# Merging two partial attentions in SBUF on GpSimd, with the opening's work and loads in a new order

## The chip, the cores and the metric

The kernel runs on one core of a Trainium2 chip. The core has five engines, each of which executes its own stream of instructions in order: PE (TensorE, matrix products into PSUM), ACT (ScalarE, functions such as Exp), DVE (VectorE), POOL (GpSimd) and SP (SyncE, which here issues every DMA). They meet only through semaphores. The metric is the time of one launch on the device, in microseconds.

## The reference, cut to what matters

Two identical layers, each an attention block and a feed-forward block, on x of 2048 rows by 512 columns in bfloat16:

```python
def _A_ref(x, wqkv, wo):              # H = 32 heads of 16
    q, k, v = split(x @ wqkv)
    p = softmax(q @ k.T / 4)
    return (p @ v) @ wo
def _B_ref(x, w1, b1, w2, b2):        # feed-forward width 1376
    y = layernorm(x)
    return gelu(y @ w1 + b1) @ w2 + b2

x = x + A(layernorm(x)); x = x + B(layernorm(x))
x = x + A(layernorm(x)); x = x + B(layernorm(x))
```

The heavy part is Exp over 32 heads x 2048 x 2048 scores in each of the two layers.

## The kernel before

**A planner writes the streams.** Nothing is looped on the chip. `Sched` and `Prog` run while the program is built: jobs are Python generators that yield tasks (an engine, a priority, a list of instructions with resources read and written, and a modelled duration). The planner keeps a modelled clock, takes for each engine the ready task of lowest priority number, and appends it to that engine's stream. The order so found is fixed; on the chip an engine that meets a wait stops, with everything behind it. A DMA is modelled with a short issue time and 2 us to landing unless given otherwise. Where the model sees a gap on PE, `fill_pe` puts in dummy matmuls of zeros (L853).

**Stages.** x is cut into 16 tiles of 128 rows and 4 chunks of 512 (`qc`). The layers are L = 1 and 3. For each row tile `job_qkv_tile` normalizes x into `xn` (L657), turns it by a DMA transpose into `xnT` (L684), and multiplies it by the three column blocks of `wqkv` (L709). K goes through a DMA transpose into `KT` (L697), V into `V` by ACT or DVE (L736, L738), Q into the DRAM buffer `q_scr` (L777). Squares and sums of q and k (L752, L753), and five short GpSimd instructions for a square root (L763 to L767), fill a bound on the scores into a spare column of q. In the tiles 0 to 3 of L = 1 ("start") the first 128 columns of q also go by a DMA transpose to `qraw` (L775). `job_qt` scales a `qraw` block to `QT` (L823).

**Attention.** `flow_scores` goes through segments: a chunk of queries, a group of four heads (`hg`, 8 of them), and a set of key tiles. A group of score tiles of 128 keys x 512 queries is written to PSUM (L915), ACT takes Exp over two or three of them into `PT` (L921), and PE multiplies `V` with them into one accumulator bank (`ACCB`, L1040). In the wide mode, which begins with the second pass over chunk 0, some tiles have their Exp done on DVE instead: `take_d` gives one to the DVE lane (L932, then `job_d`, L999 to L1002). `job_segend` turns the accumulator into `accT` (two buffers, L1067).

**Two parts.** Chunk 0 of each layer is done in two passes over the eight head groups, so that Exp can begin before all keys exist: in L = 1 over key tiles 0 to 3 and then 4 to 15, in L = 3 over 0 to 11 and then 12 to 15. After the first pass, 16 x 17 float32 numbers of each of 128 partitions are stored from `accT` into the DRAM buffer `m_scr` (L1082). After the second they are loaded into `MA` (one buffer, L1092), scaled by a weight `dw`, which is an Exp of the difference of two bounds (L1090), and added to `accT`, both on DVE (L1093, L1094). Then come the reciprocal (L1097), the product into `ob` (L1102), a transpose into `OT` (L1104), the output projection with `wo` (L1121) and the feed-forward block (`job_post`, `job_ffn`).

**The opening.** `build_startup` puts down the x and `wqkv` loads in one go (five DMAs of x and three of `wqkv`, L563 and L566), constants, and the zero and one columns of all six q/k buffers on GpSimd. `build_startup_late` then appends to GpSimd's stream the fills of `wo`, `V`, `vst`, `ob`, `b1s`, `w2` and `g10` (L606 to L613) ahead of anything a job puts there, and submits the loads of `wo`, `w1`, `w2`, b1 and b2 to SP at the lowest priority (L618 to L631). b1 is loaded element by element into a column layout.

Of the kernel before, what the change touches and what calls it, by code (L numbers as in the profile page):

```python
# [8 lines left out]
BF16 = mybir.dt.bfloat16  # L9
# [398 lines left out]
DTAIL = 16  # L408


class Builder:
# [35 lines left out]
    def alloc(self, es):  # L447
# [8 lines left out]
        self.b1s = t("b1s", [128, NFC], BF16)  # L456
# [31 lines left out]
        self.MA = t("MA", [128, 1, 16, 17], F32)  # L488
# [4 lines left out]
        self.sq = t("sq", [128, 64, 16], BF16)  # L493
# [19 lines left out]
        self.m_scr = nc.dram_tensor("m_scr", [2, 8, 128, 272], F32, kind="Internal").ap()  # L513
# [11 lines left out]
        pl["qk"] = Pool(range(6))  # L525
        pl["vst"] = Pool(range(2))
        pl["xn"] = Pool(range(3))
        pl["xnT"] = Pool(range(3))
        pl["sq"] = Pool(range(1))
        pl["n2"] = Pool(range(2))  # L530
        pl["accT"] = Pool(range(2))
        pl["MA"] = Pool(range(1))
        pl["ob"] = Pool(range(2))
# [10 lines left out]
    def qkr(self, s):  # L544
        return ("qk", s) if s < 2 else ("h", s - 2)
# [10 lines left out]
    def build_startup(self):  # L556
# [25 lines left out]
        pool(lambda e: e.iota(self.ioe[:, :, :], [[-4, 8], [-1, 4]], base=0, channel_multiplier=1, allow_small_or_imprecise_dtypes=True), [("ioe",)])  # L582
        dve(lambda e: e.memset(self.zw[:, :], 0.0), [], [("zw",)], 0.2)
        dve(lambda e: e.memset(self.ps[:, ACCB, :], 0.0), [], [("ps", ACCB)], 0.6)
        for b in range(6):
            qv = self.qks(b).rearrange("p k (h c) -> p (k h) c", c=32)
            pool(lambda e, qv=qv: e.memset(qv[:, :, 16:32], 0.0), [self.qkr(b)], 0.7)
            pool(lambda e, b=b: e.memset(self.qks(b)[:, 1, :].rearrange("p (h c) -> p h c", c=32)[:, :, 16:17], 1.0), [self.qkr(b)], 0.2)
# [11 lines left out]
    def build_startup_late(self):  # L600
        NFC = self.NFC
        n0 = self.now0
        nc = self.nc
        nfull = NFC - 1
        pool = lambda fn, writes, dur=0.4: n0("pool", I(fn, [], writes, dur))
        pool(lambda e: e.memset(self.wo[:, :, :].rearrange("p a b -> p (a b)").bitcast(F32), 0.0), [("wo0",)], 2.5)  # L606
        vv = self.V[:, :, :, :, :].rearrange("p g k h d -> p (g k h) d")
        pool(lambda e: e.memset(vv[:, :, 16:17], 1.0), [("V", hg, kb) for hg in range(8) for kb in range(16)], 1.0)
        pool(lambda e: e.memset(self.vst[:, :, :].rearrange("p s (h d) -> p (s h) d", d=17)[:, :, 16:17], 1.0), [("vst", 0), ("vst", 1)], 0.4)
        pool(lambda e: e.memset(self.ob[:, :, :], 0.0), [("ob", 0), ("ob", 1)], 1.0)  # L610
        pool(lambda e: e.memset(self.b1s[:, :], 0.0), [("b1z",)])
        pool(lambda e: e.memset(self.w2[:, nfull, :], 0.0), [("w2z",)], 0.6)
        pool(lambda e: e.memset(self.g10[:, :], 0.0), [("g10",)], 0.6)  # L613
        self.S_.submit(Task("dve", 4.0, [I(lambda e: e.memset(self.g10[96:97, :], 1.0), [], [("g10",)], 0.5)]))
        wor = self.A_wo.rearrange("(g h d) n -> h d g n", h=4, d=16)
        late = []
        for hp in range(4):
            late.append(I(lambda e, hp=hp: e.dma_start(self.wo[32 * hp:32 * hp + 16, :, :], wor[hp]), [("wo0",)], [("wo", hp)], 0.1))  # L618
        late.append(I(lambda e: e.dma_start(self.w1[:, :, :], self.B_w1.rearrange("(c p) n -> p c n", p=128)), writes=[("w1",)], dur=0.1, lat=5.0))
        late.append(I(lambda e: e.dma_start(self.w2[:, 0:nfull, :], self.B_w2[0:nfull * 128, :].rearrange("(c p) n -> p c n", p=128)), writes=[("w2", 0)], dur=0.1, lat=5.0))  # L620
        late.append(I(lambda e: e.dma_start(self.w2[0:self.FLAST, nfull, :], self.B_w2[nfull * 128:self.F, :]), [("w2z",)], [("w2", 1)], 0.1))
        late.append(I(lambda e: e.dma_start(self.w2[96:97, nfull, :], self.B_b2.rearrange("(o n) -> o n", o=1)), [("w2z",)], [("w2", 2)], 0.1))
        b1v = self.B_b1

        def ld_b1a(e):
            with nc.allow_non_contiguous_dma(reason="tiny bias load"):
                return e.dma_start(self.b1s[:, 0:nfull], b1v[0:nfull * 128].rearrange("(c p) -> p c", p=128))

        def ld_b1b(e):
            with nc.allow_non_contiguous_dma(reason="tiny bias load"):  # L630
                return e.dma_start(self.b1s[0:self.FLAST, nfull:nfull + 1], b1v[nfull * 128:self.F].rearrange("(p c) -> p c", c=1))  # L631
        late.append(I(ld_b1a, [("b1z",)], [("b1s", 0)], 0.1))
        late.append(I(ld_b1b, [("b1z",)], [("b1s", 1)], 0.1))
        for k, x in enumerate(late):
            self.S_.submit(Task("sp", 4.0, [x]), cb=(lambda: self.S_.mark(("b1ld",))) if k == len(late) - 1 else None)
        self.S_.when([("b1ld",)], lambda: self.S_.submit(Task("dve", 4.0, [I(lambda e: e.tensor_copy(out=self.b1c[:, :], in_=self.b1s[:, :]), [("b1s", 0), ("b1s", 1)], [("b1c",)], 0.2)])))
# [38 lines left out]
    def job_qkv_tile(self, L, tt, slot, i, left, prio, what):  # L675
        S_ = self.S_
        xr = yield ("get", "xn")
        xnr = self.xn[:, xr, :]
        yield self.ln_apply(tt, slot, i, xnr, ("xn", xr), prio)
# [3 lines left out]
        xs = yield ("get", "xnT")  # L683
        yield self.dma(lambda e: e.dma_start_transpose(self.xnT[:, xs, :, :], xnr), [("xn", xr)], [("xnT", xs)], prio, 0.9)  # L684
        S_.release("xn", xr)
        direct = (L == 1) or tt >= 12
        start = (L == 1 and tt < 4)
        qs = yield ("get", "qk")
        QR = self.qkr(qs)
# [5 lines left out]
        def kstore():  # L695
            if direct:
                yield self.dma(lambda e: e.dma_start_transpose(self.KT[:, :, tt * 128:(tt + 1) * 128], self.qks(qs)[:, 1, :]), [QR], [("kt", hg, tt) for hg in range(8)], prio, 1.75)  # L697
            else:
                yield self.dma(lambda e: e.dma_start(self.k_scr[tt * 128:(tt + 1) * 128, :], self.qks(qs)[:, 1, :]), [QR], [("kscr", tt)], prio)
            S_.mark(("ks", L, tt))  # L700
# [6 lines left out]
        def mm(which, b):  # L707
            for c0 in (0, 2):
                yield Task("pe", prio, [I(lambda e, c=c: e.matmul(self.ps[:, b, :], lhsT=self.xnT[:, xs, c, :], rhs=self.wqkv[:, c, which * 512:which * 512 + 512], start=(c == 0), stop=(c == 3)),  # L709
                                          [("wqkv", which), ("xnT", xs)], [("ps", b)], 0.216, [("ps", b)]) for c in (c0, c0 + 1)])  # L710
        yield ("ready", "pe", [("xnT", xs)])
        if "k" in what:
            b = yield ("get", "mb")
            yield from mm(1, b)
            yield Task("dve", prio, [I(lambda e, b=b: e.tensor_copy(out=kdst, in_=heads(self.ps[:, b, :])), [("ps", b)], [QR], 0.68)])
            S_.release("mb", b)
            S_.spawn(kstore(), prio)
        if "q" in what:
            b = yield ("get", "mb")
            yield from mm(0, b)  # L720
            qsrc = heads(self.ps[:, b, :])
            if start:
                yield Task("act", prio, [I(lambda e: e.activation(out=qdst, in_=qsrc, func=ACTF.Copy, scale=0.25 * YU), [("ps", b)], [QR], 0.65)])
            else:
                yield Task("dve", prio, [I(lambda e: e.tensor_scalar(out=qdst, in0=qsrc, scalar1=0.25 * YU, scalar2=None, op0=ALU.mult), [("ps", b)], [QR], 0.68)])
            S_.release("mb", b)
# [18 lines left out]
        S_.release("xnT", xs)  # L745
        ss = yield ("get", "sq")
# [5 lines left out]
        yield Task("dve", prio, [I(lambda e: e.tensor_tensor(out=self.sq[:, h0:h1, :], in0=v4, in1=v4, op=ALU.mult), [QR], [("sq",)], 0.12 + 0.0085 * N)])  # L752
        yield Task("dve", prio, [I(lambda e: e.tensor_reduce(out=self.n2[:, ns, h0:h1], in_=self.sq[:, h0:h1, :], axis=AX.X, op=ALU.add), [("sq",)], [("n2", ns)], 0.12 + 0.017 * N)])  # L753
# [4 lines left out]
        if "q" in what:  # L758
# [9 lines left out]
                                        [RA], [QR], 0.4)])  # L768
# [3 lines left out]
        if "q" in what:  # L772
            li = L // 2
            if start:
                yield self.dma(lambda e: e.dma_start_transpose(self.qraw[:, 0:1, tt * 128:(tt + 1) * 128], self.qks(qs)[:, 0, 0:128]), [QR], [("qraw", 0)], prio, 0.25)  # L775
                S_.mark(("q0", tt))
            yield self.dma(lambda e: e.dma_start(self.q_scr[li, tt * 128:(tt + 1) * 128, :], self.qks(qs)[:, 0, :]), [QR], [("qscr", L, tt)], prio)  # L777
            S_.mark(("qst", L, tt))
# [534 lines left out]
```

## Time and profile before

| what | value |
|---|---|
| time of a launch, median of 3 | 1919.53 us (1917.12 to 1921.61) |
| the profiled launch | 1914.84 us |
| its span, first to last instruction | 1913.1 us |
| mean granted TensorE clock | 0.983 |
| PE, DVE, POOL busy | 91%, 84%, 6% of the span |

The profiled launch is one execution; its span lacks 1.74 us of that launch's own time, and the launch lies 4.69 us under the median of the timed runs. A row of the timeline reads: start, duration, engine, line, instruction, tile written and tile read, count, and in brackets the engine's idle time before it and what ended it. SPq rows are DMA issues. In the chain of waits a DMA row runs from issue to landing. Matmul ends are modelled, and a matmul's duration overlaps with its neighbours'.

### The profile page before, as it was taken

What the parts mean: (1) busy time and instruction counts of PE and PEld (TensorE: products, weight loads), DVE (VectorE), ACT (ScalarE), POOL (GpSimd) and SP (SyncE); (2) the same over time, 40 slices, a digit from 0 to 9 for tenths busy, and PEclk for the clock granted to TensorE, in tenths of its full rate; (3) what the DMA queues carried; (4) which work ended last, traced back from release to release, by engine and by line L of the source; (5) the groups of instructions that cost most, each with busy time, mean ns of one, the idle gap of its engine ahead of it and who ended that gap; (6) DMA issues with size and microseconds to landing.
All of it is one profiled execution on the core that took longest, in us unless ns stands there. A gap on an engine that the chain in (4) does not pass through costs nothing.

```text
span 1913.1 us, 32397 instructions
## 1 busy us (share of the span) xinstructions
PE 1743.7 (91%) x13118; PEld 671.1 (35%) x13118; DVE 1600.0 (84%) x2511; ACT 1734.6 (91%) x1531; POOL 122.2 (6%) x230
## 2 busy tenths in 40 slices
PE   2879889999999999999999989999999999999997
PEld 1223333333333333333333324333333333333334
DVE  4659889989997999879988878888999798997982
ACT  1669889998999999999999989999999999999992
POOL 4102110001000020001000001000000000000000
PEclk9989999999999999999999989999999999999999
DMA  7791120102000110001611141100000000000000
GB/s 186 93 77 34 40 51 23 23 4 59 20 7 15 31 48 7 15 7 51 102 32 26 16 50 40 30 17 17 4 7 18 12 9 7 7 18 14 1 2 22
DMA packets 184515, 59.38 MB, mean 31 GB/s; under 512 B 167121, under 2 KB 178226, under 8 KB 184370
## 3 DMA queue, kind: packets, MB, share of 16 engines
q1 hardware_dynamic: 184370, 57.31, 16.1%
q8 instruction: 107, 1.75, 0.4%
q14 instruction: 38, 0.31, 0.1%
HBM read 10.92 MB, written 17.53 MB: 15 GB/s over the span
## 4 chain that ended last, share of the span: by engine, by line
ACT 51%; PE 34%; DVE 6%; DMA 6%; POOL 1%; issue 1%; SPq 0%; POOLq 0%; DVEq 0%
ACT PT L921 48%; PE ps L915 10%; PE ps L1040 6%; PE ps L853 5%; PE ps L1153 4%; PE ps L1121 3%; PE ps L709 3%; PE ps L1187 3%; DMA xnT<-xn 2%; ACT h L1180 2%; DVE dt L932 1%; DMA yT<-xn 1%; DMA b1s<-in_B_b_dram 1%; DVE de L1002 1%; DMA MA<-m_scr 1%
## 5 line engine op out<-in xcount | busy, mean ns | idle before, releaser
L921 ACT ACTIVATE PT<-ps 128x1024 bf16<-128x1024 f32 (+1 forms) x1466 | 1666.1, 1293 | 100.4 <-PE ps L915 96.3
L915 PE MATMUL ps<-QT,KT 32*128 32x512 bf16 x4096 | 600.3, 385 | 81.0 <-ACT PT L921 56.1
L853 PE MATMUL ps<-wqkv,zw 128*128 128x256 bf16 x3574 | 530.0, 277 | 0.0
L1040 PE MATMUL ps<-PT,V 128*17 128x512 bf16 x3632 | 435.3, 387 | 10.5 <-DVE accT L1067 10.0
L932 DVE TENSOR_SCALAR dt<-ps 128x512 int32<-128x512 f32 x464 | 317.6, 685 | 129.7 <-PE ps L915 126.8
L853 PEld LDWEIGHTS ps<-wqkv,zw 128*128 128x128 bf16 x3574 | 298.9, 98 | 211.9 <-issue 175.6
L915 PEld LDWEIGHTS ps<-QT,KT 32*128 32x128 bf16 x4096 | 163.5, 91 | 504.3 <-issue 301.7
L1002 DVE SCALAR_TENSOR_TENSOR de<-dt,dv 128x1024 uint16<-128x1024 int32 (+1 forms) x246 | 284.0, 1155 | 2.3
L999 DVE SCALAR_TENSOR_TENSOR de<-dt 128x1024 bf16<-128x1024 uint16 (+1 forms) x246 | 283.7, 1153 | 2.3
L1040 PEld LDWEIGHTS ps<-PT,V 128*17 128x17 bf16 x3632 | 103.2, 87 | 248.2 <-issue 207.0
L709 PE MATMUL ps<-wqkv,xnT 128*128 128x512 bf16 x384 | 113.1, 405 | 54.9 <-DMA xnT<-xn 50.2
L1001 DVE TENSOR_TENSOR dv<-de,dv 128x1024 f16<-128x1024 bf16 (+1 forms) x246 | 159.7, 650 | 2.3
L1000 DVE TENSOR_SCALAR dv<-dt 128x1024 bf16<-128x1024 uint16 (+1 forms) x246 | 160.0, 651 | 0.0
L1040 PE MATMUL ps<-de,V 128*17 128x512 bf16 x464 | 138.0, 384 | 1.3 <-DVE accT L1067 1.0
L1153 PE MATMUL ps<-yT,w 128*128 128x512 bf16 (+1 forms) x352 | 100.7, 394 | 9.9 <-DMA yT<-xn 8.5
L652 POOL TENSOR_SCALAR rs<-mv 128x4 f32<-128x4 f32 (+1 forms) x19 | 10.2, 539 | 1328.8 <-DVE mv L645 1328.5
L1187 PE MATMUL ps<-w,h 128*128 128x512 bf16 x280 | 75.4, 382 | 0.4
L1067 DVE STREAM_TRANSPOSE accT<-ps 128x512 f32<-128x512 f32 x80 | 56.8, 710 | 18.0 <-PE ps L1040 15.0
L1121 PE MATMUL ps<-wo,OT 128*128 128x512 bf16 x256 | 68.2, 382 | 0.2 <-DVE xres L1123 0.2
L1173 DVE TENSOR_SCALAR h<-ps,b1c 128x512 f32<-128x512 f32 (+1 forms) x77 | 56.9, 738 | 13.7 <-PE ps L1153 12.4
L709 PEld LDWEIGHTS ps<-wqkv,xnT 128*128 128x128 bf16 x384 | 29.0, 100 | 102.9 <-issue 56.5
L1153 PEld LDWEIGHTS ps<-yT,w 128*128 128x128 bf16 (+1 forms) x352 | 26.8, 102 | 52.3 <-issue 29.4
(97 smaller groups left out, 719.3 us busy)
## 6 DMA issues: line engine op xcount, KB each, us to landing
q_scr<-qk SPq DMA_DIRECT2D x22, 256.0 KB, 2.0
k_scr<-qk SPq DMA_DIRECT2D x12, 256.0 KB, 2.0
q_scr<-h SPq DMA_DIRECT2D x10, 256.0 KB, 2.2
m_scr<-accT SPq DMA_DIRECT2D x16, 136.0 KB, 9.4
MA<-m_scr SPq DMA_DIRECT2D x16, 136.0 KB, 2.4
out_dram<-xres SPq DMA_DIRECT2D x16, 128.0 KB, 1.7
v_scr<-vst SPq DMA_DIRECT2D x12, 136.0 KB, 1.7
V<-v_scr SPq DMA_DIRECT2D x8, 204.0 KB, 4.5
```

What stands on the lines that cost most here:

```text
L709: yield Task("pe", prio, [I(lambda e, c=c: e.matmul(self.ps[:, b, :], lhsT=self.xnT[:, xs, c, :], rhs=self.wqkv[:, c, which * 512:which * ...
L853: P.op("pe", lambda e: e.matmul(self.ps[:, b, 0:FILL_N], lhsT=self.zw[:, :], rhs=self.wqkv[:, 0, 0:FILL_N], start=st, stop=st, skip_group_ ...
L915: ops.append(I(lambda e, hp=hp, hg=hg, kb=kb, q=q, b=b: e.matmul(self.ps[:, b, :], lhsT=self.KT[32 * hp:32 * hp + 32, hg, kb * 128:(kb + 1 ...
L921: S_.submit(Task("act", 1e-5 * gi, [I(lambda e, pt=pt, n=n, b0=b0: e.activation(out=self.PT[:, pt:pt + n, :], in_=self.ps[:, b0:b0 + n, :] ...
L932: S_.submit(Task("dve", 0.0, [I(lambda e, ds=ds, w=w: e.tensor_scalar(out=self.dt32[:, ds, w * 512:(w + 1) * 512], in0=self.ps[:, DLANE, : ...
L999: yield Task("dve", pr, [I(lambda e: e.scalar_tensor_tensor(out=E, in0=lo, scalar=65536.0, in1=lo, op0=ALU.subtract, op1=ALU.mult), RT, [( ...
L1000: yield Task("dve", pr, [I(lambda e: e.tensor_scalar(out=v, in0=lo, scalar1=CUB_B * sc / 65536.0, scalar2=CUB_A * sc, op0=ALU.mult, op1=AL ...
L1001: yield Task("dve", pr, [I(lambda e: e.tensor_tensor(out=D, in0=E, in1=v, op=ALU.mult), [("de", es), ("dv", s)], [("dv", s)], 0.12 + 0.521 ...
L1002: yield Task("dve", pr, [I(lambda e: e.scalar_tensor_tensor(out=Pb, in0=t32, scalar=2.0 ** -9, in1=D, op0=ALU.mult, op1=ALU.subtract), RT ...
L1040: ops.append(I(lambda e, hp=hp, hg=hg, kb=kb, ap=ap, first=first: e.matmul(self.ps[32 * hp:32 * hp + 17, ACCB, :], lhsT=self.V[:, hg, kb, ...
L1153: yield Task("pe", pr, [I(lambda e, c=c: e.matmul(self.ps[0:M, b, :], lhsT=self.w1[:, c, fc * 128:fc * 128 + M], rhs=self.yT[:, c, :], sta ...
L1187: yield Task("pe", pr, [I(lambda e, fc=fc, i=i, b=b: e.matmul(self.ps[:, b, :], lhsT=self.gt(fc, i), rhs=self.w2[:, fc, :], start=(fc == 0 ...
```

## The change

- After the first pass GpSimd copies the 16 x 16 numerators into the `OT` block of that head group (unused until then; in L = 3 only once the output projection of the last chunk of L = 1 has read it) and the denominators into a new `den`. After the second pass GpSimd does the scaling and the two additions in place. `m_scr` and `MA` are gone.
- SP issues `wqkv`'s key block second. x tiles 4 to 7 are loaded after K of tile 1 is stored, tiles 8 to 15 after K of tile 3.
- GpSimd fills only two q/k buffers at first, DVE a third and the one column of `V`. All other fills are jobs of the lowest priority that run in GpSimd's gaps. The loads of `wo`, `w1` (now 4 DMAs), `w2` (now 2 and two small ones) and b1 come after all K and V of L = 1. b1 is loaded in rows and turned by PE.
- In tiles 0 to 3 of L = 1: `xn` and `xnT` live in buffers not yet in use (`de`, `yT`), one for each tile; ACT squares q and k, instead of DVE; the first 128 columns of q are transposed by PE into a PSUM bank, which L823 reads. For all tiles q and k of a buffer are separate resources in the planner, and there are three `sq` buffers.
- Planner: the filler on PE is allowed from the start, with the zero weights as its moving data until `wqkv` is there; the DVE lane's last tiles of a segment have priority 0.5 instead of 2.5; a group of P·V products is formed only from tiles that end within 1.2 us, and only one group is outstanding until each of a segment's four heads has its first.

```diff
         ldx(0, 1)
+        ldw(1, 512)
         ldx(1, 2)
         ldx(2, 4)
-        ldw(1, 512)
         ldw(0, 0)
         ldw(2, 1024)
-        ldx(4, 8)
-        ldx(8, 16)
+        self.S_.when([("ks", 1, 1)], lambda: ldx(4, 8))
+        self.S_.when([("ks", 1, 3)], lambda: ldx(8, 16))
...
-        for b in range(6):
-            qv = self.qks(b).rearrange("p k (h c) -> p (k h) c", c=32)
-            pool(lambda e, qv=qv: e.memset(qv[:, :, 16:32], 0.0), [self.qkr(b)], 0.7)
-            pool(lambda e, b=b: e.memset(self.qks(b)[:, 1, :].rearrange("p (h c) -> p h c", c=32)[:, :, 16:17], 1.0), [self.qkr(b)], 0.2)
+        pads("pool", 0)
+        pads("pool", 1)
+        pads("dve", 2)
+        dve(lambda e: e.memset(vv[:, :, 16:17], 1.0), [], [("V", hg, kb) for hg in range(8) for kb in range(16)], 0.7)
...
+        def fills():
+            for b in range(3, 6):
...
+                S_.release("qk", b)
...
+            yield ("keys", [("kv", 1, tt) for tt in range(self.NT)])
+            ld = lambda fn, reads, writes: self.dma(fn, reads, writes, 4.0, 0.4, 5.0)
...
+        S_.spawn(fills(), 4.0)
...
             if start:
-                yield self.dma(lambda e: e.dma_start_transpose(self.qraw[:, 0:1, tt * 128:(tt + 1) * 128], self.qks(qs)[:, 0, 0:128]), [QR], [("qraw", 0)], prio, 0.25)
+                yield Task("pe", 0.5, [I(lambda e: e.transpose(self.psbf(self.q0bank)[:, tt * 128:(tt + 1) * 128], self.qks(qs)[:, 0, 0:128], self.ident[:, :]), [QQ, ("ident",)], [("ps", self.q0bank)], 0.1, [("ps", self.q0bank)])])
...
-        pr = 2.5
+        pr = lambda: 0.5 if len(bt["tiles"][0][0]["todo"]) < DURGE else 2.5
...
-            if self.pv_out >= 2 or not sg["rdy"]:
+            if self.pv_out >= (1 if self.pv_first else 2) or not sg["rdy"]:
...
-            for it in sg["rdy"]:
+            near = [it for it in sg["rdy"] if self.P.last_writer[it[2]].t1 <= S_.now + PV_NEAR]
...
+            for it in near:
...
-            yield self.dma(lambda e: e.dma_start(ms, T[:, :, 0:17]), [RA], [("mscr", hg)], 1.2)
+            if L == 3:
+                yield ("keys", [("oproj", 1, self.NC - 1)])
+            yield Task("pool", 1.2, [I(lambda e: e.tensor_copy(out=M, in_=T[:, :, 0:16]), [RA], [RO], 0.5), I(lambda e: e.tensor_copy(out=den, in_=T[:, :, 16]), [RA], [RD], 0.2)])
...
-            m = yield ("get", "MA")
-            yield self.dma(lambda e: e.dma_start(self.MA[:, m, :, :], ms), [("mscr", hg)], [("MA", m)], 1.2)
-            yield Task("dve", 1.2, [I(lambda e: e.tensor_tensor(out=self.MA[:, m, :, :], in0=self.MA[:, m, :, :], in1=dw.unsqueeze(2).broadcast_to([128, 16, 17]), op=ALU.mult), [RW, ("MA", m)], [("MA", m)], 0.44)])
-            yield Task("dve", 1.2, [I(lambda e: e.tensor_tensor(out=T[:, :, 0:17], in0=T[:, :, 0:17], in1=self.MA[:, m, :, :], op=ALU.add), [("MA", m), RA], [RA], 0.44)])
+            yield Task("pool", 1.2, [I(lambda e: e.tensor_tensor(out=M, in0=M, in1=dw.unsqueeze(2).broadcast_to([128, 16, 16]), op=ALU.mult), [RW, RO], [RO], 0.75),
+                                     I(lambda e: e.tensor_tensor(out=den, in0=den, in1=dw, op=ALU.mult), [RW, RD], [RD], 0.2),
+                                     I(lambda e: e.tensor_tensor(out=T[:, :, 16], in0=T[:, :, 16], in1=den, op=ALU.add), [RD, RA], [RA], 0.2),
+                                     I(lambda e: e.tensor_tensor(out=T[:, :, 0:16], in0=T[:, :, 0:16], in1=M, op=ALU.add), [RO, RA], [RA], 0.75)])
```

More of the change, by code (lines that the diff above doesn't have):

```diff
@@ L682, in job_qkv_tile @@
             S_.release("lnc", slot)
[L683 to L687, printed above, removed]
+        if not start:
+            xs = yield ("get", "xnT")
+            xnT, RXT = self.xnT[:, xs, :, :], ("xnT", xs)
+        yield self.dma(lambda e: e.dma_start_transpose(xnT, xnr), [RX], [RXT], prio, 0.9)
+        if not start:
+            S_.release("xn", xr)
         qs = yield ("get", "qk")
-        QR = self.qkr(qs)
+        QQ, QK = ("qk", qs, 0), ("qk", qs, 1)
         heads = lambda ap: ap.rearrange("p (h d) -> p h d", d=16)
@@ L744, in job_qkv_tile @@
             S_.release("mb", b)
-        S_.release("xnT", xs)
-        ss = yield ("get", "sq")
+        if not start:
+            S_.release("xnT", xs)
+        if not start:
+            ss = yield ("get", "sq")
         ns = yield ("get", "n2")
@@ L1166, in job_ffn @@
         tiles = list(range(4 * qc, 4 * qc + 4))
-        yield ("keys", [("retq", k) for k in range(2, 6)])
+        yield ("keys", [("retq", k) for k in range(2, 6)] + [("rets", k) for k in (1, 2)])
         for fc in range(NFC):
```

209 lines of the change are left out of this document (128 added, 81 removed).

## The prediction

> **What bounds the kernel now.** I read the page first, then what ACT waits for, then two stretches of the windows view.
>
> ```profile
> PE 1743.7 (91%) x13118; PEld 671.1 (35%) x13118; DVE 1600.0 (84%) x2511; ACT 1734.6 (91%) x1531; POOL 122.2 (6%) x230
> ```
>
> ```profile
> ACT PT L921 <- PE ps L915: 96.3, 107, 8.6
> ACT L723 <- DMA KT<-qk: 35.4, 1, 35.4
> ACT h L1230 <- PE ps L1153: 32.4, 10, 21.3
> ```
>
> ```profile
> 0.00:54.20 54.20, 18.38 (x79) 8.36 (x80) 23.44 (x59) 5.76 (x10) 23.24 (x57) 0.97 0.74 181
> 54.20:144.50 90.30, 72.08 (x425) 21.93 (x423) 54.32 (x128) 61.97 (x64) 4.61 (x7) 0.91 0.88 81
> ```
>
> ACT is busy for 1734.6 us of 1913.1 us, so the time is ACT's fixed work plus 178.5 us in which it idles. PE's share counts the planner's dummy matmuls, so it says little. The idle time sits in three places: before the first Exp at 54.20; in the first pass of chunk 0, 54.20 to 144.50, where ACT works 61.97 of 90.30 us (28.3 idle; after the length stand the busy times of PE, PEld, DVE, ACT and POOL with their counts, then the granted clock, the DMA share and GB/s); and in the tail (32.4), which the change leaves alone. The opening in order of time, then a step of the chain of waits:
>
> ```profile
> 8.10 1.88 POOL L606 MEMSET wo<- 128x2048 f32 x1
> ...
> 14.37 0.46 POOL L652 TENSOR_SCALAR rs<-mv 128x1 f32<-128x1 f32 x2
> ...
> 14.91 1.10 POOL L653 TENSOR_TENSOR rs<-rs,cneg 128x1 f32<-128x1 f32 x2
> ...
> 23.25 8.95 SPq L684 DMA_TRANSPOSE xnT<-xn  x3
> ...
> 29.61 1.86 PE L709 MATMUL ps<-wqkv,xnT 128*128 128x512 bf16 x4 [29.61 <-DMA xnT<-xn]
> ...
> 44.17 0.60 ACT L723 ACTIVATE h<-ps 128x512 bf16<-128x512 f32 x1 [1.46 <-PE ps L709]
> ...
> 54.20 6.52 ACT L921 ACTIVATE PT<-ps 128x1024 bf16<-128x1024 f32 x7 [8.56 <-PE ps L915]
> ```
>
> ```profile
> 17.24 11.84 DMA b1s<-in_B_b_dram
> ```
>
> The first normalization waits on GpSimd behind the fills until 14.37. Its transpose then queues on SP behind the weight loads until 23.25, and the data come only after the element-wise b1 loads. The first projection starts at 29.61. The first pass, by ACT's longest waits, the chain, and the issues:
>
> ```profile
> 94.12 1.02 ACT L921 ACTIVATE PT<-ps 128x1024 bf16<-128x1024 f32 x1 [5.54 <-PE ps L915]
> ...
> 123.37 1.02 ACT L921 ACTIVATE PT<-ps 128x1024 bf16<-128x1024 f32 x1 [8.06 <-PE ps L915]
> ...
> 144.53 4.86 ACT L921 ACTIVATE PT<-ps 128x1536 bf16<-128x1536 f32 x4 [5.25 <-PE ps L915]
> ```
>
> ```profile
> 73.07 9.87 DMA m_scr<-accT
> ...
> 113.82 7.86 DMA xnT<-xn
> ```
>
> ```profile
> m_scr<-accT SPq DMA_DIRECT2D x16, 136.0 KB, 9.4
> ...
> xnT<-xn SPq DMA_TRANSPOSE x44, 2.5
> ```
>
> A store of 136 KB that takes 9.4 us, eight times in this pass, fills the DMA engines: a transpose issued at 113.82 lands after 7.86 us instead of 2.5, PE stands in order before its matmul, and ACT behind PE.
>
> **The change part by part.** *Opening.* Rows for its steps:
>
> ```profile
> 3.53 1.03 POOL L587 MEMSET h<- 128x1024 bf16 x1
> ...
> 3.87 0.71 DVE L598 CAST sel<-m 32x4 bf16<-32x4 f32 x1
> ...
> 5.43 1.29 DVE L644 BATCH_NORM_STATS2 st<-xres 128x6 f32<-128x512 bf16 x2
> ...
> 9.93 2.26 POOL L608 MEMSET V<- 128x512 bf16 x1
> ...
> 38.16 0.68 DVE L752 TENSOR_TENSOR sq<-qk 128x1024 bf16<-128x1024 bf16 x1
> ...
> 50.09 0.33 POOL L767 TENSOR_SCALAR h<-qt 128x32 bf16<-128x32 f32 x1 [0.70 <-DMA KT<-h]
> ```
>
> ```profile
> 50.64 2.27 DMA qraw<-h
> ```
>
> GpSimd is free of its first constants and two buffers near 3.7. DVE's own constants ended at 4.58; it gains a buffer's pads (1.2 by GpSimd's row) and V's ones (at most 2.26), so its first statistics start by 6 to 8. Statistics take 0.65, the aggregate and the normalization together as much again (an estimate from that row), the two GpSimd steps 0.8 with up to one fill in front of them (1.0), the transpose 2.5. The first projection comes at about 12 instead of 29.61: 17.6 less. From there to the last q of the four tiles took 14.6 us; four tiles' transposes no longer wait for free buffers or behind K's, so I take 12.5: 2.1 less. From that q to the first Exp took 10.0. Out go the squares on DVE (0.68), the wait for K's transpose (0.70) and the q transpose by DMA (2.27); in comes a PE transpose, 0.5 by the first projection's 1.86 for four: 3.2 less. ACT's extra squares, eight of about 0.60 like its copy at 44.17, fit where ACT idled for 35.4 us. First Exp near 31.3, **-23**. Bounds: -17 (fills and the 2 MB of x and weight loads each hold the first transpose some 3 us longer) to -27. The filler, allowed from the start, can overrun its modelled gap; it costs within that lower bound.
>
> *First pass.* The three waits that stand behind late transposes sum to 18.9 of the 28.3 us idle. Without the stores the copy to `OT` and `den` costs GpSimd a microsecond or two, and `accT` comes free sooner. I take 90% of the 18.9: **-17**, from -8 (new lateness, below) to -23.
>
> *Second merge, both layers.*
>
> ```profile
> L1093 DVE TENSOR_TENSOR MA<-MA,dw x16: 426/442/443, 206.3 to 1229.1; 128x272 f32<-128x272 f32 x16
> L1094 DVE TENSOR_TENSOR accT<-accT,MA x16: 399/432/439, 207.3 to 1230.6; 128x272 f32<-128x272 f32 x16
> ```
>
> ```profile
> 250.72 2.37 DMA MA<-m_scr
> ...
> 1102.20 7.71 DMA KT<-qk
> ```
>
> ```profile
> L763 POOL TENSOR_TENSOR qt<-n,qy x32: 251/506/1197, 40.5 to 1155.7; 128x32 f32<-128x32 f32 x32
> ```
>
> ```profile
> ACT PT L921 <- PE ps L915: 18.8, 9, 5.3
> ...
> ACT PT L921 <- PE ps L915: 18.3, 20, 2.8
> ```
>
> The last two rows are ACT's waits in 144.5 to 300 (13.5 without the one at 144.53) and in 1000 to 1250. In both, the chain runs through DMAs of the merge or a transpose beside a store (7.71 us for K's at 1102.20, issued just after a store). I let 40% of the 31.8 go: -13. DVE loses 16 x (0.44 + 0.43) = 14 us of work. It gains a wait: the reciprocal stands in DVE's stream behind GpSimd's four steps, modelled at 1.9 us. GpSimd shows no such 256-element step. Below, a memset bounds it (1.03 for 1024 columns, so 0.3); above, eight times the slowest 32-element row, 9.6. Nearest is the median, 0.506 for 32 elements, mostly fixed cost; I take 1.2 for each of the two large steps and 0.5 for each small one, 3.4 in all, 1.5 over the model. Sixteen times that is 24 us of DVE waiting, with a DVE that has 16% to spare and PE and ACT buffered by `PT`; I charge a fifth, +5. In sum **-8**, from -14 to +83 (the upper bound's price is worked out among the rivals).
>
> The Trainium skill, "SBUF — State Buffer", section "Who interferes with whom", speaks against this move: a GpSimd instruction and a VectorE instruction with two SBUF inputs share a port pair that one holds for its whole length while the other stands still. The spread of L763 (251 to 1197 ns for one shape) agrees with it. By the page "GPSIMD Engine Reference", section 3.1, a float32 add of 2048 columns takes 4497 ns on GpSimd; an estimate from it for 256 columns is 0.56 us, by which the merge would stay within the model and the sum be 5 us better.
>
> *Weights behind keys and values.*
>
> ```profile
> 10.31 6.41 SPq L618 DMA_DIRECT2D wo<-in_A_wo_dram x4
> ...
> L1121 PE MATMUL ps<-wo,OT x256: 379/379/390, 330.5 to 1874.6; 128*128 128x512 bf16 x128
> ```
>
> `wo` is first read at 330.5, long after the last K. The cover is the second pass, whose q blocks are fetched segments ahead. But SP's issue (6.41 for `wo`, and about as much again for the rest, an estimate by the number of DMAs) now stands before q transposes and the late q tiles' `xnT`. Nothing to 6 us; I take **+2**.
>
> *Order of the DVE lane and of P·V.* The waits it can touch:
>
> ```profile
> ACT PT L921 <- PE ps L915: 19.8, 34, 3.3
> ...
> ACT PT L921 <- PE ps L915: 8.1, 20, 0.8
> ```
>
> These are 300 to 1000 and 1250 to 1867: 27.9 us in 54 short waits. Better ends of segments could save some; one outstanding group at a segment's start could cost some. **0**, from -10 to +8.
>
> Sum: -23 - 17 - 8 + 2 + 0 = -46. The profiled launch took 1914.84, so it would take 1868.8; the median of the runs lies 4.69 higher, and from it I get 1919.53 - 46 = 1873.5, call it **1873**.
>
> **The rivals.**
>
> *The first pass finds a new lateness (20%).*
>
> ```profile
> 113.82 1.26 SPq L684 DMA_TRANSPOSE xnT<-xn  x1
> ```
>
> For it: twelve x, twelve K and some sixteen q transposes at 1.26 us of issue or more on one SP queue are 50 us in a pass that should take 73; DVE has 54.32 us of work there. Against it: both fit. Then half of the idle stays, -8 for -17, with an opening of -20: 1885.
>
> *GpSimd's merge is slow (10%).* GpSimd's steps and the lane's two-input DVE instructions hold each other up, as L763's spread suggests: each large step takes 2.5 us, the merge 6. DVE then waits 4 us sixteen times, 64 us; longer waits outlast the buffers, so a third reaches ACT: +21 for +5, 1889. This is the rule of the State Buffer page of the Trainium skill cited above.
>
> *Slower than before (3%).* The same place, at the price of the upper bound: the reciprocal holds DVE for longer than the PT buffers and the lane bear. With large steps of 9.6 us a merge takes about 20, DVE waits 18, and a third of that reaches ACT sixteen times, 96 us for +5: 1964. It overtakes the 51 us of the other terms when a merge costs ACT over 3.2 us: at that third a DVE wait of 9.6, a large step of 5.3. Against it: `accT` has two buffers, and the planner puts other work ahead of the reciprocal.
>
> *The reordering does less than it says (7%).* The fills only move: GpSimd takes one ahead of each step of the root, SP's loads still stand ahead of the transposes, and the first Exp comes at 42. Then -12 for -23: 1884.
>
> *More goes than I count (10%).* All DMA-caused waits go and half of the 27.9 too: 1853.
>
> **How the numbers follow.** The forecast holds 50%, with 1863 to 1882 as its own range. From the terms' bounds, not all at one end, and the rivals up to 1889, I give 1850 to 1893; about 8% lies above, 6% below by more than that. A measurement of this kernel tells about 0.2% (4 us) from no change. Slower 3%, within 0.2% 1%, faster 96%.
>
> **What would show it.** First projection near 12, first Exp near 31, first 1536-column Exp near 104; no wait over 3 us behind `xnT` in the first pass; GpSimd's 256-element steps near 1.2 us; reciprocals of the merged segments waiting about 1.5 us for GpSimd; the tail's 32.4 unchanged. A first Exp past 37, or steps of over 2.5 us, makes the prediction wrong; so does a change of over 10 us in the 27.9.

## The result, and the profile after

| | before | after |
|---|---|---|
| time of a launch, median of 4 | 1918.32 us (1915.75 to 1921.61) | 1853.64 us (1853.01 to 1855.89) |
| span of the profiled launch | 1913.1 us | 1851.3 us |
| mean granted clock | 0.983 | 0.995 |

The ratio is 0.9664, with a 95% interval of 0.9646 to 0.9682: 64.7 us less, where 46 were forecast. The time lies inside the stated range, 1850 to 1893, and some 9 us under the forecast's own, 1863 to 1882. The profile's page of the changed kernel begins so (busy time and share by engine); below it are ACT's longest waits:

```profile
PE 1723.7 (93%) x13057; PEld 664.7 (36%) x13057; DVE 1590.1 (86%) x2469; ACT 1737.9 (94%) x1539; POOL 171.1 (9%) x324
```

```profile
ACT PT L973 <- PE ps L967: 55.7, 95, 6.9
ACT h L1293 <- PE ps L1216: 32.5, 10, 21.3
ACT sq L752 <- DVE qk L750: 12.6, 1, 12.6
```

ACT does the same work (1734.6 us before, 1737.9 now), so the gain is idle time: 1851.3 - 1737.9 = 113.4 for 178.5. Its wait for PE's scores fell from 96.3 to 55.7 and the opening's 35.4 to 12.6; the tail stayed at 32.5. The opening and the first pass, in the timeline and by windows (length; busy us of PE, PEld, DVE, ACT, POOL; granted clock; DMA share; GB/s):

```profile
7.68 0.46 POOL L678 TENSOR_SCALAR rs<-mv 128x1 f32<-128x1 f32 x2 [1.68 <-DVE mv L671]
...
9.35 5.43 SPq L718 DMA_TRANSPOSE yT<-de  x4
...
12.01 1.44 PE L742 MATMUL ps<-wqkv,yT 128*128 128x512 bf16 x3 [12.01 <-DMA yT<-de]
...
29.98 10.19 ACT L973 ACTIVATE PT<-ps 128x1024 bf16<-128x1024 f32 x11 [4.97 <-PE ps L967]
44.27 1.02 ACT L973 ACTIVATE PT<-ps 128x1024 bf16<-128x1024 f32 x1 [4.10 <-PE ps L967]
...
108.68 2.36 ACT L973 ACTIVATE PT<-ps 128x1536 bf16<-128x1536 f32 x2 [6.87 <-PE ps L967]
```

```profile
0.00:29.98 29.98, 17.18 (x93) 8.60 (x94) 20.49 (x52) 9.79 (x18) 19.29 (x55) 1.00 0.75 197
29.98:108.68 78.70, 70.25 (x421) 21.50 (x419) 55.79 (x133) 61.66 (x65) 9.16 (x23) 0.95 0.56 110
```

GpSimd's two steps no longer stand behind fills (7.68 for 14.37), the first transpose is issued at 9.35 for 23.25, and the first Exp comes at 29.98 for 54.20. The first pass lasts 78.70 for 90.30; its 17.0 us of idle sit mostly at 44 and at 108.68, the switch to the second part. The merge on GpSimd, and who waits for its last step; then ACT's waits in 110 to 250, 250 to 950, 950 to 1190 and 1190 to 1805:

```profile
L1155 POOL TENSOR_TENSOR OT<-OT,dw x16: 621/714/1431, 166.1 to 1160.3; 128x256 f32<-128x256 f32 x16
```

```profile
L1158 POOL TENSOR_TENSOR accT<-accT,OT x16: 728/732/1584, 167.4 to 1162.6; 128x256 f32<-128x256 f32 x16
...
  DVE rv L1160: 3.6, 5
```

```profile
ACT PT L973 <- PE ps L967: 10.6, 8, 6.9
...
ACT PT L973 <- PE ps L967: 15.2, 35, 1.5
...
ACT PT L973 <- PE ps L967: 4.3, 12, 0.6
...
ACT PT L973 <- PE ps L967: 12.3, 24, 0.8
```

The four windows stand for those of the prediction, moved to where the stages now lie. The first holds the 6.87 of the switch, so 3.7 remain of 13.5; the third keeps 4.3 of 18.3. The other two together hold 27.5 where they held 27.9.

By stages, span against span (cut at the first Exp, at the first 1536-column Exp and at the end of the last Exp; the last two rows are runs of the next section):

| | opening | first pass | rest of Exp | tail | span |
|---|---|---|---|---|---|
| before | 54.20 | 90.3 | 1722.0 | 46.6 | 1913.1 |
| after | 29.98 | 78.7 | 1696.0 | 46.6 | 1851.3 |
| difference | -24.2 | -11.6 | -26.0 | 0 | -61.8 |
| merge alone | 52.66 | 72.6 | 1716.8 | 46.1 | 1888.1 |
| all but the merge | 31.48 | 111.3 | 1713.3 | 46.5 | 1902.5 |

### The profile page after: what moved, and what is told of

Same layout as the page of the kernel before. It is cut to its first block, busy times and chain, and to the rows that moved or that the text cites. A ratio compares the mean times of both kernels' runs of the same rounds, so it can differ in the third digit from the quotient of the medians.

```text
span 1851.3 us, 32298 instructions
## 1 busy us (share of the span) xinstructions
PE 1723.7 (93%) x13057; PEld 664.7 (36%) x13057; DVE 1590.1 (86%) x2469; ACT 1737.9 (94%) x1539; POOL 171.1 (9%) x324
## 4 chain that ended last, share of the span: by engine, by line
ACT 53%; PE 36%; DVE 6%; DMA 2%; issue 1%; POOL 1%; SPq 0%; POOLq 0%; DVEq 0%
ACT PT L973 50%; PE ps L967 11%; PE ps L1099 7%; PE ps L905 5%; PE ps L1216 4%; PE ps L742 4%; PE ps L1250 3%; PE ps L1184 3%; ACT h L1243 2%; DMA xnT<-xn 1%; DVE dt L984 1%; DMA yT<-xn 1%; DVE de L1054 1%; DVE de L1051 1%; ACT L973 0%
## 5 line engine op out<-in xcount | busy, mean ns | idle before, releaser
L973 ACT ACTIVATE PT<-ps 128x1024 bf16<-128x1024 f32 (+1 forms) x1466 | 1665.0, 1289 | 59.8 <-PE ps L967 55.7
L905 PE MATMUL ps<-wqkv,zw 128*128 128x256 bf16 x3508 | 518.8, 275 | 0.0
L905 PEld LDWEIGHTS ps<-wqkv,zw 128*128 128x128 bf16 x3508 | 289.7, 98 | 208.2 <-issue 176.2
L742 PE MATMUL ps<-wqkv,xnT 128*128 128x512 bf16 x336 | 95.4, 391 | 8.8 <-DMA xnT<-xn 8.0
L1099 PEld LDWEIGHTS ps<-de,V 128*17 128x17 bf16 x463 | 31.5, 87 | 40.0 <-issue 31.3
L1216 PEld LDWEIGHTS ps<-yT,w 128*128 128x128 bf16 (+1 forms) x352 | 27.6, 101 | 50.8 <-issue 25.7
```

The costliest lines, as they stand in the source:

```text
L905: P.op("pe", lambda e: e.matmul(self.ps[:, b, 0:w], lhsT=self.zw[:, :], rhs=rhs, start=st, stop=st, skip_group_check=True), [("zw",), R], ...
L973: S_.submit(Task("act", 1e-5 * gi, [I(lambda e, pt=pt, n=n, b0=b0: e.activation(out=self.PT[:, pt:pt + n, :], in_=self.ps[:, b0:b0 + n, :] ...
L1099: ops.append(I(lambda e, hp=hp, hg=hg, kb=kb, ap=ap, first=first: e.matmul(self.ps[32 * hp:32 * hp + 17, ACCB, :], lhsT=self.V[:, hg, kb, ...
L1216: yield Task("pe", pr, [I(lambda e, c=c: e.matmul(self.ps[0:M, b, :], lhsT=self.w1[:, c, fc * 128:fc * 128 + M], rhs=self.yT[:, c, :], sta ...
```

## The experiments

My theory after the result: the gain behind the opening comes from the DRAM route's end, not from where the merge's arithmetic runs, and it was undersized. The rivals: GpSimd is what helps, by unloading DVE; the weights' late loads or the planner's rules do it.

**The merge alone.** The kernel before, with only this of the change:

```diff
-            yield self.dma(lambda e: e.dma_start(ms, T[:, :, 0:17]), [RA], [("mscr", hg)], 1.2)
+            yield Task("pool", 1.2, [I(lambda e: e.tensor_copy(out=M, in_=T[:, :, 0:16]), [RA], [RO], 0.5), I(lambda e: e.tensor_copy(out=den, in_=T[:, :, 16]), [RA], [RD], 0.2)])
...
-            yield self.dma(lambda e: e.dma_start(self.MA[:, m, :, :], ms), [("mscr", hg)], [("MA", m)], 1.2)
...
+                                     I(lambda e: e.tensor_tensor(out=T[:, :, 0:16], in0=T[:, :, 0:16], in1=M, op=ALU.add), [RO, RA], [RA], 0.75)])
```

> The kernel before with the merge in SBUF on GpSimd alone; opening, loads and planner rules as before. Theory (the DRAM stores caused the lateness): the first Exp stays at 54.2 us; in the first pass the waits of 5.5, 8.1 and 5.3 us go, and with them most of the 13.5 and 18.3 us of waits around the two merges: 35 to 43 us less than before, ratio 0.978 to 0.982. Rival (the transposes' own queue makes them late, the stores only lie beside it): at most 12 us less, ratio 0.994 or more.

Measured: 1892.46 us, ratio 0.9871 (0.9828 to 0.9915), some 25 us less, where 35 to 43 were expected. Its windows, then the switch to the second part of the keys in its timeline:

```profile
0.00:52.66 52.66, 17.78 (x79) 8.16 (x80) 23.03 (x59) 5.76 (x10) 23.23 (x57) 0.97 0.71 186
52.66:125.28 72.62, 67.99 (x425) 21.59 (x423) 54.64 (x128) 61.60 (x64) 9.09 (x23) 0.98 0.43 88
```

```profile
123.04 0.18 PE L794 MATMUL ps<-krhs,sel 32*128 32x8 bf16 x1 [1.98 <-DVE krhs L792]
...
125.28 2.37 ACT L919 ACTIVATE PT<-ps 128x1536 bf16<-128x1536 f32 x2 [5.42 <-PE ps L913]
```

The same work in the first pass now takes 72.62 for 90.3: 17.7 less, with DMA engines busy 0.43 for 0.88 of it. Two of the prediction's three waits stood behind the stores: those of 5.54 and 8.06 are gone, and the longest left between the first Exp and the switch is 1.32. The third did not: at the switch ACT waits 5.42 without the stores, for 5.25 with them. No late transpose holds PE there now. It waits for a bound over the new keys (`krhs`), which steps on DVE, GpSimd and PE work out one after the other. The shorter waits made up the rest, 3.9 us. In the rest of Exp the merge alone brings only 5.3, so the expected end of most of the 13.5 and 18.3 did not come.

**All but the merge.** The changed kernel, with the store, the load and DVE's two steps put back (the same lines, reversed).

> The changed kernel with only the store to DRAM, the load back and the merge on VectorE put back. Theory: the first Exp stays at 30 us, the first pass again has waits of 5 to 8 us behind late transposes, and 35 to 45 us of the 64.7 us gained are lost: ratio to before 0.985 to 0.990. Rival (the gain around the merges comes from the planner's new rules for the lane and for P.V): 12 us or less are lost, ratio 0.973 or less.

Measured: 1904.51 us, ratio 0.9933 (0.9914 to 0.9952). More is lost than the 35 to 45 expected, some 50 of the 64.7. The first pass by windows, and steps of the chain in it (start, length):

```profile
31.48:142.73 111.25, 82.54 (x422) 22.43 (x420) 55.76 (x133) 62.45 (x65) 4.62 (x7) 0.76 0.86 86
```

```profile
66.64 8.97 DMA xnT<-xn
82.55 10.13 DMA m_scr<-accT
...
112.45 9.68 DMA xnT<-xn
```

```profile
71.19 0.72 DVE L1129 STREAM_TRANSPOSE accT<-ps 128x512 f32<-128x512 f32 x1 [11.16 <-DMA m_scr<-accT]
...
71.96 0.61 PE L1101 MATMUL ps<-PT,V 128*17 128x512 bf16 x4 [8.78 <-DVE accT L1129]
...
73.50 1.02 ACT L975 ACTIVATE PT<-ps 128x1024 bf16<-128x1024 f32 x1 [8.96 <-PE ps L969]
```

The opening is 22.7 us shorter than before the change, and by the end of the first pass, which takes 111.25, all but 1.8 of this is gone. The transposes issued at 66.64 and 112.45 take 9 to 10 us beside stores (issued in the 8 us before them); the loads of `wo` and `w1` are issued only from 128.35 on, so these two don't stand behind them. The pass's longest wait has another cause, shown by the last three rows: a store holds its `accT` buffer, one of two, until it has landed; DVE stands 11.16 us for the buffer, PE behind DVE, and ACT 8.96 behind PE. In all DVE waits 13.6 us for stores in this pass, and 1.0 in the kernel before the change. That goes some way to explain why the pass is 21 us longer than before; the rest is not settled. The two halves bring some 25 and 13 us, the whole 64.7: they are not terms that add. With the stores back, the opening's gain is lost in the first pass.

**The merge's arithmetic on DVE.**

```diff
-                                     I(lambda e: e.tensor_tensor(out=T[:, :, 0:16], in0=T[:, :, 0:16], in1=M, op=ALU.add), [RO, RA], [RA], 0.75)])
+                                     I(lambda e: e.tensor_tensor(out=T[:, :, 0:16], in0=T[:, :, 0:16], in1=M, op=ALU.add), [RO, RA], [RA], 0.44)])
```

The task goes to `"dve"` instead of `"pool"`, with all four steps and DVE's times.

> The changed kernel with the four merge steps of each head group on VectorE instead of GpSimd, still in SBUF (the copy after the first pass stays on GpSimd). Theory (what counts is that nothing goes through DRAM): within 4 us of the changed kernel, ratio to before 0.965 to 0.969. Rival (VectorE's relief of 14 us is worth its time): 8 us or more slower than the changed kernel, ratio 0.970 or more. Rival (GpSimd's steps hold VectorE up): faster than the changed kernel by 4 us or more.

Measured: 1853.85 us, ratio 0.9673 (0.9623 to 0.9723). The ratio's interval is wide because the runs of the kernel before scatter; the four runs themselves lie between 1852.26 and 1855.42 us, beside 1853.64 of the changed kernel. The engine makes no difference that can be seen; "unloading DVE" falls. This run and the one before it were taken on one chip, and both do the arithmetic on DVE. They differ in the way through DRAM: 1904.51 against 1853.85, so in the changed kernel that way costs 50.7 us.

**A longer merge.** After the scaling, five doublings and one multiplication by 1/32 on GpSimd, told to the planner as taking no time, then at their length:

```diff
+  *[I(lambda e: e.tensor_tensor(out=M, in0=M, in1=M, op=ALU.add), [RO], [RO], 0.0) for _ in range(5)],
+  I(lambda e: e.tensor_scalar(out=M, in0=M, scalar1=1.0 / 32, scalar2=0.0, op0=ALU.mult, op1=ALU.add), [RO], [RO], 0.0),
```

> The changed kernel with six more GpSimd steps of 256 elements in each of the sixteen merges (five doublings and a product with 1/32, which leave the values as they were), modelled at nothing, so that the planner's order is the same to the instruction. At 0.6 to 0.7 us each a merge takes some 4 us more. By the prediction's rate (a third of VectorE's wait reaches ScalarE): about 64 us of waits at the reciprocals and 21 us more in all. Theory now (the buffers and the planner's order take up waits of this size): 2 to 8 us more.

> The kernel with the long merge (each merge's numerators doubled five times on GpSimd and then divided by 32, some 3.5 us more in each of 16 merges), with the added steps told to the planner at 0.61 and 0.40 us instead of about nothing. With untold steps it took 57.5 us more than the changed kernel. If the price comes from work that the planner had not reckoned with, so that VectorE stands at the reciprocal's wait with the evictions behind it, a planner that knows the 3.5 us puts VectorE's steps elsewhere: at most 10 to 15 us over the changed kernel, and a wait of the reciprocal for GpSimd under 15 us in all. If the chain through accT, accumulator banks and P.V order carries the price itself, it stays above 35 us.

Measured: 1911.16 us (0.991, from 0.989 to 0.993) untold; 1880.59 us (0.9802, from 0.9786 to 0.9818) told. On the chip of the told run the unaltered changed kernel took 1853.02 us (0.9655, from 0.9642 to 0.9668); on that of the untold run it was not taken:

> The changed kernel itself, unaltered, on this chip: 0.964 to 0.968 of the kernel before, as measured at first (0.9664). It serves as the ground on which the next three runs are read.

The added steps, and the reciprocal's wait, untold and then told:

```profile
L1157 POOL TENSOR_TENSOR OT<-OT x80: 605/612/1474, 165.3 to 1219.8; 128x256 f32<-128x256 f32 x80
```

```profile
  DVE rv L1162: 48.1, 15
```

```profile
L1157 POOL TENSOR_TENSOR OT<-OT x80: 605/784/1657, 162.8 to 1193.5; 128x256 f32<-128x256 f32 x80
```

```profile
  DVE rv L1162: 13.8, 11
```

Untold, 5 x 0.612 + 0.404 (the multiplication's median) = 3.46 us for each of 16 merges, 55 in all, cost 57.5 against the first measurement of the changed kernel. By the ratios to the kernel before on each chip (0.991 and 0.9664) it is 47. So little or nothing is absorbed, and both expected numbers, 2 to 8 and 21, are missed by far. (The planner puts a little time between steps even so, and the order differed from the first merge on, which that expectation did not allow for.) Told, the cost is 27.6, between the two theories' numbers: about half of it was the planner's ignorance. The other half remains although DVE's wait is down to 13.8, and what carries it is not shown.

**Weights later, and earlier.** The loads of `wo`, `w1`, `w2` and b1 held until a part of chunk 0's second pass is done; or not held at all.

```diff
-            yield ("keys", [("kv", 1, tt) for tt in range(self.NT)])
+            yield ("keys", [("ot", 1, 0, 2)])
```

> The changed kernel with the loads of wo, w1, w2 and the biases held until the third head group of the second pass is done, instead of until all keys and values of the first layer exist. Theory (the 6.9 us wait at 108.7 us is a transpose late behind those loads): that wait falls below 2 us and the time by 5 to 7 us, ratio to before 0.963. Rival (the wait is the switch to groups of three tiles, or moves to another transpose): no change, 0.966 to 0.967.

> The changed kernel with the loads of wo, w1, w2 and the biases issued at once instead of behind the keys and values; b1 still in rows. Theory: some 2.9 MB stand ahead of or beside the first transposes, as before the change, the first projection comes 6 to 12 us later, the wait at the start of the second pass falls to 4.4 us, and the time is 4 to 10 us above the changed kernel. Rival (the element-wise b1 loads alone made the opening late): the first projection stays within 2 us of 12.0 and the time falls by 1 to 3 us.

Measured: later, 1856.12 us (0.968, from 0.9638 to 0.9723); earlier, 1863.5 us (0.9662, from 0.9642 to 0.9683, against runs of the kernel before that were longer on that chip: 1926.15). SP at the switch in the changed kernel, and the chain there:

```profile
98.65 1.75 SPq L644 DMA_DIRECT2D wo<-in_A_wo_dram  x4
100.44 0.91 SPq L647 DMA_DIRECT2D w<-in_B_w_dram  x2
101.45 1.20 SPq L718 DMA_TRANSPOSE xnT<-xn  x1
```

```profile
101.45 5.54 DMA xnT<-xn
```

The transpose lands 5.54 us after its issue beside the weights. Held longer, the switch's wait falls from 6.87 to 4.44 and no further, but one of 4.07 appears at 161 and the end does not move: the rival held. Issued early, they still come behind GpSimd's fills, from 18.17 on, when the first transposes (issued at 9.34) are out. So the run puts nothing ahead of those, the first projection stays at 11.99 and the first Exp comes at 30.14, and neither the theory nor the rival on the opening is tested by it. The loads cost some 10 us against the first measurement, 5.7 of them by the switch, which comes at 114.34: a wait of 9.42 stands at 47.0, behind a store to `q_scr` issued after the weights at 35.08 that took 7.93 us. By the ratio, against the longer runs on that chip, nothing is lost; so this price is uncertain.

**The fills first.** GpSimd's low-priority fills put ahead of the jobs again, in the changed kernel (`fills()` appended at once).

> The changed kernel with all of GpSimd's fills put ahead of the jobs in its stream, as before the change. GpSimd is then busy to about 14 us instead of about 4 before the first root. Theory (without the DRAM stores the first pass has room, so the opening's delay reaches the end whole): first projection at 18 to 20 us, first Exp at 36 to 38, and the time 5 to 8 us above the changed kernel, ratio to before about 0.970. Rival (the first pass takes the delay up, since keys and values then run ahead): within 2 us of the changed kernel.

Measured: 1853.41 us, ratio 0.9614 (0.9588 to 0.964) on that chip. First projection at 15.79, first Exp at 34.16, 4.2 later; the first pass is 73.67 and the switch comes at 107.83. The delay is smaller than expected and the first pass takes it up, as the rival had it. So up to 4 us of the opening's gain is slack. Of the 17.6 us by which the first projection came earlier, the fills are worth 3.8; which of the moved loads brought the rest was not tested one by one.

**The planner's rules undone.**

```diff
-DURGE = 8
-PV_NEAR = 1.2
+DURGE = 0
+PV_NEAR = 1e9
```

> The changed kernel with the lane's priority constant at 2.5 and every finished tile allowed into a P.V group (the limit of one outstanding group at a segment's start stays). Theory (the planner's rules are worth about nothing, as forecast): within 4 us of the changed kernel. Rival (the gain around the merges and in the long stretch from 300 us on is theirs): 8 us or more above it.

Measured: 1861.71 us (1856.15 to 1866.75), ratio 0.9652 (0.9622 to 0.9682); span 1857.3 for 1851.3, of it 8.5 in the rest of Exp. The fills' run on that chip took 1853.41, so the two rules may be worth 4 to 8 us; the median is 8.1 above the first measurement of the changed kernel, at the edge of the rival, while the ratio (0.9652 for 0.9664) shows no loss. The next runs differ by as much with no rule touched, so this isn't settled.

**Half of x later.** Tiles 12 to 15 loaded one key tile later, with the merge on GpSimd, then on DVE.

```diff
-        self.S_.when([("ks", 1, 3)], lambda: ldx(8, 16))
+        self.S_.when([("ks", 1, 3)], lambda: ldx(8, 12))
+        self.S_.when([("ks", 1, 4)], lambda: ldx(12, 16))
```

> The changed kernel, with the second half of the load of x's tiles 8 to 15 started one key tile later, and the job of the last chunk's rows behind it. Theory: in the first pass of the changed kernel the waits of 4.10, 1.02 and 1.34 us at 44 to 49 us stand behind the first xnT, which the store to q_scr (3.88 us where others take about 2) and the load of qraw (4.91) have made late because 1 MB of x is under way beside them. Then a smaller load takes 2 to 5 us from these waits and from the end: 1849 to 1852 us by the first measurement, a ratio 0.001 to 0.003 under that of the unaltered changed kernel. Rival: those waits are set by the chain of layer norm, store and transposed load itself, or the time comes back at the switch to the second part of the keys; then no change within 2 us.

> The later load of x together with the merge's steps on VectorE. VectorE's merge alone made no difference (0.9673 against 0.9664), so this should stand with the run of the later load alone, within 2 us. If VectorE's merge is better once the first pass has fewer waits, it is 1 to 3 us under it.

Measured: 1859.54 us (0.9691, from 0.9677 to 0.9704) and 1864.9 us (0.9718, from 0.97 to 0.9736). With the later load the store to `q_scr` takes 2.00 and the waits near 45 are gone in the first of the two, as the theory had it. (In the unaltered repeat on the same chip the store took 3.43 and the first of these waits only 1.64.) But the time comes back, with more: ACT's waits in 100 to 250, unaltered and with the later load, are

```profile
ACT PT L973 <- PE ps L967: 13.6, 11, 7.6
```

```profile
ACT PT L974 <- PE ps L968: 20.4, 8, 11.7
```

The rival's second reason held, the time comes back at the switch (11.65 for 7.59 there), but not its "no change": 6.5 us are lost. The second run missed its number by 5 us although moving the merge cost nothing by itself. These edits, each of which makes the planner write another order, cost from nothing to 12 us. That the order itself does this, and not the edit's own effect, is not shown. No version here has a median under 1853 us.

## Why the prediction was right, and where it was not

- **Opening, -23: right.** -24.2, by the steps named: first projection at 12.01 for "about 12", from there 11.4 us to the last q for 12.5, then 6.6 to the first Exp for 6.8, which comes at 29.98 for 31.3.
- **First pass, -17: two of three waits rightly read, size not.** The merge alone brings 17.7, but the match is partly luck: of the 18.9 us only 5.54 and 8.06 stood behind the stores (seven of the eight are issued in this pass). The 5.25 at the switch I put down to a late transpose, and it stays at 5.42 without the stores, or 4.44 where the weights are held longer, since PE must then wait for the bound over the new keys. Shorter waits brought what was missing. In the changed kernel 11.6 arrive. A wait of 4.10 is new, at the end of a chain of the store to `q_scr` (3.88), the load of `qraw` (4.91) and `xnT` (2.55), and the switch takes 6.87, behind an `xnT` late beside the weights; I expected none over 3 behind `xnT`. The rival with a new lateness had 8. Splits of this pass differ by run (76.3 in the unaltered repeat, 78.7 here) at the same total.
- **Second merge, -8: mis-sized, and most of the error.** I let 40% of the 31.8 us of waits go and charged 5 for DVE's new wait. 13.5 - 3.7 and 18.3 - 4.3 make 23.8, 75%; DVE's wait is 3.6 in all, not 24, since the large steps take 0.71 and 0.73 and not the 1.2 that I took from a 32-element row. But -23.8 isn't the merge's own: alone it brought 5.3 in the whole rest, all but the merge brought 8.7, and together they bring 26.0. Put the other way round, taking the way through DRAM out is worth 17.3 in the rest (1713.3 to 1696.0) where all else is changed, and 5.3 where nothing else is. What these 12 us of difference hang on is not settled. Undoing two of the planner's three rules takes 8.5 back.
- **Weights, +2: near.** They cost 2.4 at the switch (6.87 for 4.44 in the run with the later loads), and holding them longer gains nothing.
- **Order of the DVE lane and P·V, 0: not told apart.** The 27.9 became 27.5; undoing two of the rules cost 4 to 8 us by the times and nothing by the ratio, in the bounds given.
- **The sum.** -24.2 - 11.6 - 23.8 - 0.4 = -60.0 of the span's -61.8. What failed is the assumption that the terms are separate: -23 for the opening holds only if the stores go, since the first pass without that gives it all back.
- **The rivals.** "More goes than I count" gave 1853, the time measured, by luck. Its own parts make more: 2 beyond the 17, 19 beyond the 13 and half of the 27.9 are 35 us, so 1838 and not 1853. And the measured gain has other parts: it had all of the waits behind DMAs and half of the 27.9 going, and neither went so far. GpSimd's merge was not slow: single large steps took up to 1.43 and 1.58 us, but DVE waited only 3.6 in all. The slower case had the right place and the wrong price: a third of DVE's wait was to reach ACT, with the turn at 9.6 us of wait for each merge. In the long merge DVE waited (48.1 - 3.6) / 16 = 2.8 us more each and the kernel paid 57.5 / 16 = 3.6 (2.9 by the ratios). At that rate the whole gain is spent with some 4 to 5 us added to a merge, if the planner doesn't know of them.
- **The length of a large step.** The estimate from the Trainium skill, page "GPSIMD Engine Reference", section 3.1, 0.56 us for a large step, was nearer than my 1.2; the runs show 0.71 and 0.73 here and 0.61 in the doublings.

## What to carry to other kernels

A small store can cost by what queues beside it and by the buffer that it holds. Here 136 KB took 9.4 us to land where a store of 256 KB to `q_scr` took 2.0; transposes beside it landed after 8 to 10 us for 2.5, and it holds the buffer that it reads (DVE waited 1.0 us for that in the first pass before the change, and 13.6 with the new opening). Seven such stores in the first pass make some 14,400 DMA packets (40,183 with them, 25,755 in the run of the merge alone), about 68 bytes each; that the short packets make it slow was not tested. So look at the landing time of the other transfers in a stretch. Terms that fill the same stretch need not add: here an earlier start was worth almost nothing where the next stage's transfers then collided. When a step goes into an order that is planned ahead, its modelled length should be right: here steps that the planner didn't know of cost 47 to 57 us for 55 of work, and half as much once it knew them.

## What the runs showed of the hardware

**GpSimd's steps take longer beside a working VectorE.** With DVE mostly standing at the reciprocal (untold) the doubling's median was 612 ns; with DVE working beside it (told) it was 784, at the same minimum of 605. DVE's side is smaller: its lane's step with two inputs on 1024 columns (`de<-dt,dv`) took 1230 ns in the mean told and 1215 in the unaltered repeat, and 1301 for 1209 in 104 to 300, where eight of the merges lie. Its total busy time was 1610.6 us for 1590.3, but part of that is more work, 2481 instructions for 2469. The Trainium skill, page "SBUF — State Buffer", section "Who interferes with whom", has a GpSimd instruction and certain VectorE ones take turns on a shared port pair; these rows agree. No run isolated it (the two plans differ in order too), so how much of the told merge's 27.6 us this is stays open.

**PE is slower after it has waited.** The kernel before, around the wait that ends at 94.12, in windows of 4 us (the third number from the end is the granted clock):

```profile
88.00:92.00 4.00, 0.00 (x0) 0.00 (x0) 0.00 (x0) 0.57 (x1) 0.00 (x0) 0.79 1.03 199
92.00:96.00 4.00, 3.53 (x10) 0.77 (x10) 2.22 (x6) 1.02 (x1) 0.00 (x0) 0.50 0.60 95
96.00:100.00 4.00, 4.00 (x24) 0.95 (x22) 2.59 (x6) 2.78 (x3) 0.00 (x0) 0.86 0.88 52
100.00:104.00 4.00, 3.67 (x24) 0.97 (x24) 1.89 (x6) 3.74 (x5) 0.00 (x0) 1.00 1.31 157
```

PE does nothing in the first, works at a granted clock of 0.50 in the second, and has the full clock again in the fourth. Over the whole first pass the matmuls took 82.54 us (422) at a granted clock of 0.76 in the changed kernel with the stores put back, and 67.99 (425) at 0.98 in the run of the merge alone; the same 98 projections took 472 and 388 ns in the mean. In 1130 to 1260 the untold long merge still merges, to 1222; the changed kernel has ended its last merge at 1163, so it does other work beside. Their rows, of which a score matmul's mean, 454 and 382 ns, can be compared:

```profile
1130.00:1260.00 130.00, 113.68 (x740) 39.39 (x737) 96.69 (x158) 101.06 (x95) 54.62 (x84) 0.80 0.05 12
```

```profile
1130.00:1260.00 130.00, 123.65 (x925) 46.68 (x925) 110.08 (x175) 127.00 (x113) 15.38 (x22) 1.00 0.07 16
```

So a wait that stops PE for some microseconds costs more than its length. How much of the long merge's price this is, no run isolated. I had not put this into any term.
